# The straight turn of the inverse inside SBUF, and a last stage of 64-row, 32-column tiles, in a gated mix of an S4 convolution and a dense block

## The chip, the cores and the metric

One core of a Trainium2 chip runs the whole kernel. The metric is the device time of one execution in microseconds. Five engines work side by side, each through its own list of instructions in order: PE (products; PEld is its weight loads), DVE, ACT, POOL, and SP, which here only issues transfers. POOL issues transfers too. A transfer is asynchronous: what needs its data waits for a semaphore.

## The reference, cut to what matters

L = 2048 rows, D = 512 channels, N = 128 states, F = 1792 hidden units.

```python
g = sigmoid((u * gate_w).sum(-1, keepdims=True))
# A: S4 convolution
dt = exp(log_dt)[:, None]
K  = einsum("dn,dnl,dn->dl", Cc, exp((dt * A)[:, :, None] * arange(L)), dt * Bc).real
Yf = rfft(pad(u.T, 2 * L)) * rfft(pad(K, 2 * L))
a  = irfft(Yf, 2 * L)[:, :L].T + u * Dskip
# B: dense block
b  = gelu(u @ w1 + b1) @ w2 + b2
return g * a + (1 - g) * b
```

## The kernel before, in words

The transforms are done as products with small matrices, in three factors. The kernel has two functions with pools of their own. `front` computes the taps K, the first factors of both transforms and nearly all of the dense block; a planner orders it by due times. It leaves in DRAM `t2_d` (32 frequencies n, each a tile of 128 x 2 x 512: signal and taps after the first factors), in the output array the gated dense part of the 16 row tiles, and a list `late` of 14 entries of dense products (three PE products each) for the last two row tiles.

`conv` is written out by hand. It takes 16 steps s, two frequencies n = 2s and 2s+1 each. On PE a step issues `signal(s + 1)` (p2u), `taps(s + 2)` (p2k) and `inverse(s)` (pa); each is four products whose two tiles are halves of the array (64 columns for p2u and p2k, 64 rows for pa). ACT copies the taps out of PSUM (`k`), DVE multiplies both spectra in six operations of `product(s)` (`z`, `v`), PE's `inverse(s)` leaves one PSUM tile `pa` for each n, and `turn(s)` moves it on: ACT copies it to an SBUF tile `sa` (four of them in turn), and `settle` sends it towards `t3`, a tile of 128 partitions x 32 x 512. In `pa` the partition is the 32 places q for each of four parts j (which of two output halves, real or imaginary); in `t3` the partition is the frequency and part, with q along the free axis: 32 partitions' rows of `sa` become one row of `t3`.

Before, n = 0 to 27 go by DRAM: SP stores each `sa` to `t4_d[n]` (L1102), and after every eighth n (and after n = 27) POOL issues one gather from `t4_d` into rows of `t3` (L1105: three of 2 MB and one of 1 MB, the `GROUPS` table). The last four n go straight from `sa` to `t3`, one POOL transfer each, into four partitions 32 apart (L1107: rows 7, 39, 71 and 103 for the first).

SP's list holds, in the order of the program: the fetches of `t2` and of a matrix tile `cc` for each four n (12 tiles deep, `N_T2`), the 28 stores to `t4_d`, and from slot 32 on the loads of the dense part back into eight tiles `mo` (`dense`, in the same ring of 12).

In the last two steps there are no taps left, and `rest(4)` puts four `late` entries on PE ahead of each inverse; `rest(14)` takes what is left after the loop. Then comes the last stage: 16 row tiles t, each of two products with K = 128 rows and 64 columns (pb, L1164), one DVE operation that multiplies by the gate and adds the dense part in `mo` (L1166), and the store of two tiles at a time, of the last four singly.

Memory of the pools is handed on from `front` to `conv`: a tile that is laid over a tile of `front` waits for its last user. In PSUM, `pk` and `pa` have two buffers each, `pu` four; `pb` uses those of `pu`, `acc` of `rest` those of `pk`.

Of the kernel before, what the change touches and what calls it, by code (L numbers as in the profile page):

```python
# [9 lines left out]
F32 = mybir.dt.float32  # L10
# [3 lines left out]
ALU = mybir.AluOpType  # L14
# [3 lines left out]
P = 128  # L18
L = 2048
D = 512  # L20
# [44 lines left out]
D_COE = 0.99  # L65
D_OUT = -13.28
N_LATE = 2
N_REST = 4
N_T2 = 12
W_DVE = ((1, 0), (3, 0), (5, 0))  # L70

GROUPS = ((0, 8, 0, 4), (8, 8, 1, 4), (16, 8, 2, 4), (24, 4, 3, 8), (28, 1, 7, 32), (29, 1, 15, 32), (30, 1, 23, 32), (31, 1, 31, 32))
PI = float(np.pi)
TWO_PI = 2.0 * PI
TURN = 2.0**32
# [8 lines left out]
def slot_q():  # L84
    return [32 + m if m < 32 else 63 - m for m in range(64)]


def k0_order():
    return [8 * (n % 4) + n // 4 for n in range(32)]


def split12(v):
# [11 lines left out]
def constants():  # L104


    def om(e4):
        a = 2.0 * np.pi * (np.asarray(e4) % (4 * L)) / (4 * L)
        return np.cos(a), -np.sin(a)

    k0 = np.arange(32)
    p = np.arange(32)
    q = np.asarray(slot_q())
    k1 = np.arange(64)
    qn = np.arange(64)

    er, ei = om(4 * (64 * np.outer(p, k0) + 16 * p[:, None]))

    f1 = np.zeros((2, 32, 32, 2, 2))
    for i in range(2):  # L120
        f1[i, :, :, 0, i] = er
        f1[i, :, :, 1, i] = ei
    f1h, f1l = split12(np.concatenate([f1.reshape(64, P)] * 2, 0))


    g1 = np.zeros((2, 2, 32, 2, 32))
    for i in range(2):
        g1[i, 0, :, i] = er.T / L
        g1[i, 1, :, i] = ei.T / L
    g1 = g1.reshape(4, 32, 64)  # L130
    rows = np.zeros((P, 64))
    for first, count, at, step in GROUPS:
        for i in range(count):
            for j in range(4):
                rows[at + step * (4 * i + j)] = g1[j, k0_order()[first + i]]
    g1 = rows


    f2 = np.zeros((32, 2, 64, 2, 64))
    g2 = np.zeros((32, 2, 64, 64, 2))  # L140
    for k in range(32):
        er, ei = om(4 * (q[:, None] * k + 32 * np.outer(q, k1)) + q[:, None])
        f2[k, 0, :, 0], f2[k, 1, :, 0], f2[k, 0, :, 1], f2[k, 1, :, 1] = er, -ei, ei, er
        er, ei = om(4 * (qn[None] * k + 32 * np.outer(k1, qn)) + qn[None])
        g2[k, 0, :, :, 0], g2[k, 1, :, :, 0] = er, ei
        g2[k, 0, :, :, 1], g2[k, 1, :, :, 1] = -ei, er
    g2 = g2.reshape(32, P, 32, 2, 2).transpose(0, 1, 3, 4, 2)

    ko = k0_order()
    f2 = f2.reshape(32, P, P)[ko]  # L150
    g2 = g2[ko].reshape(16, 2, 2, 64, P).transpose(0, 2, 1, 3, 4).reshape(32, P, P)
    c2 = np.stack([f2, g2], 1).reshape(8, 4, 2, P, P).transpose(0, 3, 1, 2, 4)
    c1 = np.concatenate([f1h, f1l], 1)
    return (
        np.ascontiguousarray(c1, dtype=np.float32),
        np.ascontiguousarray(g1, dtype=np.float32),
        np.ascontiguousarray(c2, dtype=np.float32),
    )
# [105 lines left out]
def gated_mix(  # L264
# [18 lines left out]
    nc = tc.nc  # L283

    cp = ctx.enter_context(tc.tile_pool(name="cp", bufs=1))
    dr = ctx.enter_context(tc.tile_pool(name="dr", bufs=1, space=DRAM))

    dt_d = dr.tile([1, D], F32, name="dt_d")
    t2_d = dr.tile([32, P, 2, D], F32, name="t2_d")
    t4_d = dr.tile([32, P, D], F32, name="t4_d")  # L290

    half_pi = cp.tile([P, 1], F32, name="half_pi")
    nc.vector.memset(half_pi, PI / 2)
# [3 lines left out]
    gate = cp.tile([P, 2, 16], F32, name="gate")  # L297
# [731 lines left out]

    def conv(pool, ps, late):  # L1030

        t3 = pool.tile([P, 32, D], F32, name="t3", bufs=1)
        g1t = pool.tile([P, 64], F32, name="g1t", bufs=1)
        ko = k0_order()
        c4s, t2s = {}, {}

        def fetch(n):
            if n % 4 == 0:
                c4s[n // 4] = pool.tile([P, 4, 2, P], F32, tag="cc", name=f"cc{n}", bufs=3)
                nc.sync.dma_start(c4s[n // 4], c2[n // 4])  # L1040
            t2s[n] = pool.tile([P, 2, D], F32, tag="t2", name=f"t2{n}", bufs=N_T2)
            nc.sync.dma_start(t2s[n], t2_d[ko[n]])
            if n == 7:
                nc.sync.dma_start(g1t, g1)


# [19 lines left out]
        def signal(s):  # L1066
            pus[s] = []
            for c in range(2):
                pu = ps.tile([P, D], F32, tag="pu", name=f"p2u{s}{c}", bufs=4)
                pair(s, 0, c, pu)  # L1070
                pus[s].append(pu)

        def product(s):

            (ur, ui), (kr, ki) = pus.pop(s), fac.pop(s)
            z = [pool.tile([P, D], F32, tag=f"z{i}", name=f"z{s}{i}", bufs=1) for i in range(4)]
            v = [pool.tile([P, D], F32, tag=f"v{i}", name=f"v{s}{i}", bufs=2) for i in range(2)]
            nc.vector.tensor_mul(z[0], ur, kr)
            nc.vector.tensor_mul(z[1], ur, ki)
            nc.vector.tensor_mul(z[2], ui, ki)  # L1080
            nc.vector.tensor_mul(z[3], ui, kr)
            nc.vector.tensor_sub(v[0], z[0], z[2])
            nc.vector.tensor_add(v[1], z[1], z[3])
            prod[s] = v
# [10 lines left out]
                    r = slice(64 * i, 64 * i + 64)  # L1095
                    nc.tensor.matmul(pas[2 * s + i], w[r], v[c][r], start=(c == 0), stop=(c == 1))  # L1096

        def settle(n, sa):

            for first, count, at, step in GROUPS:  # L1100
                if count > 1 and first <= n < first + count:
                    nc.sync.dma_start(t4_d[n], sa)  # L1102
                    if n == first + count - 1:
                        rows = t4_d[first : n + 1].rearrange("n (j q) d -> (n j) q d", j=4)
                        nc.gpsimd.dma_start(t3[at:P:step], rows)  # L1105
                elif n == first:
                    nc.gpsimd.dma_start(t3[at:P:step], sa)  # L1107

        def turn(s):
            for n in (2 * s, 2 * s + 1):  # L1110
                sa = pool.tile([P, D], F32, tag="sa", name=f"sa{n}", bufs=4)
                nc.scalar.copy(sa, pas.pop(n))  # L1112
                settle(n, sa)

        accs, mos = {}, {}

# [18 lines left out]

        for n in range(N_T2):
            fetch(n)
        nxt = N_T2
        taps(0)
        signal(0)  # L1140
        taps(1)
        for s in range(16):

            for n in range(nxt, min(2 * s + N_T2, 40)):
                (fetch if n < 32 else dense)(n if n < 32 else n - 32)
                nxt = n + 1
            product(s)
            if s + 1 < 16:
                signal(s + 1)
            if s + 2 < 16:  # L1150
                taps(s + 2)
            else:
                rest(N_REST)
            inverse(s)
            turn(s)
        rest(14)
        for s in range(N_LATE):
            z = mos[7][:, s]
            nc.vector.scalar_tensor_tensor(z, accs[s], gate[:, 1, 14 + s : 15 + s], z, ALU.mult, ALU.add)

        for t in range(16):
            pb = ps.tile([P, D], F32, tag="pu", name=f"pb{t}", bufs=4)
            for b in range(2):
                nc.tensor.matmul(pb[64 * b : 64 * b + 64], g1t, t3[:, 2 * t + b], start=True, stop=True)  # L1164
            z, g = mos[t // 2][:, t % 2], gate[:, 0, t : t + 1]
            nc.vector.scalar_tensor_tensor(z, pb, g, z, ALU.mult, ALU.add)  # L1166
            if t >= 12:
                nc.sync.dma_start(out[t], z)
            elif t % 2 == 1:
                nc.sync.dma_start(out[t - 1 : t + 1].rearrange("s p d -> p s d"), mos[t // 2])  # L1170

    ctx.enter_context(tc.manual_schedule())
    keep = ctx.enter_context(tc.tile_pool(name="keep", bufs=1))
# [17 lines left out]
def layout(inputs):  # L1191

    x = np.asarray(inputs["A_u"]).reshape(L, D)
    xpq = x.reshape(32, 64, D)
    qs = np.asarray(slot_q())

    xl = xpq[:, qs].reshape(32, 2, 16, 2, D).transpose(2, 3, 1, 0, 4).reshape(16, P, D)

    xs = xpq.reshape(32, 16, 4, D).transpose(1, 2, 0, 3).reshape(16, P, D)
    xt = xs.reshape(NSB, SB, 4, P).transpose(0, 3, 2, 1)  # L1200

    order = np.arange(D).reshape(4, 2, NCH, 2, 8).transpose(0, 2, 3, 1, 4).reshape(D)
    names = ["A_A_re", "A_A_im", "A_B_re", "A_B_im", "A_C_re", "A_C_im"]
    prm = np.stack([np.asarray(inputs[n])[order].T for n in names], 1)
    w1 = np.asarray(inputs["B_w1"]).reshape(4, P, NF, P).transpose(2, 1, 0, 3).reshape(NF, P, D)
    c1, g1, c2 = constants()
    return {
        "xl": xl,
        "xs": xs,
        "xt": xt,  # L1210
        "prm": prm,
        "logdt": np.asarray(inputs["A_log_dt"])[order].reshape(1, D),
        "dskip": np.asarray(inputs["A_Dskip"])[order].reshape(16, 4, 8).transpose(1, 0, 2).reshape(4, P),
        "w1": w1,
        "b1": np.asarray(inputs["B_b1"]).reshape(NF, P).T,
        "w2": np.asarray(inputs["B_w2"]),
        "b2": np.asarray(inputs["B_b2"]).reshape(1, D),
        "gw": np.asarray(inputs["gate_w"]).reshape(1, D),
        "c1": c1,
        "g1": g1,  # L1220
        "c2": c2,
    }
# [24 lines left out]
```

## Time and profile before

| | us |
|---|---|
| runs | 575.47, 573.12, 574.60 (median 574.6) |
| profiled execution | 573.21 |
| its span | 571.4 |
| end of `front` on PE | 433.7 |
| last inverse (pa) | 532.24 to 534.16 |
| pb, last stage | 550.16 to 567.09 |

Share of the span: PE 95% busy, DVE 79%, ACT 63%, POOL 6%; the mean granted clock of PE is 0.975. The costliest groups of the page belong to `front`. Those of `conv`, as groups by line (line, engine, operation, out<-in, count, then busy us, mean ns of one, idle time before and its releaser):

```profile
L1112 ACT COPY sa<-pa 128x512 f32<-128x512 f32 x32 | 17.7, 588 | 36.8 <-PE pa L1096 21.1
L1055 PE MATMUL p2k<-t,cc 128*64 128x512 f32 x128 | 35.4, 613 | 3.0 <-DMA t<-t_d 1.7
```

The issues of transfers by kind on the page (line, engine, operation, count, KB each, median us from issue to landing); in such rows `t` stands for `t2` tiles and for `t3`, `t_d` for `t2_d` and `t4_d`, since the digits are left out:

```profile
t<-t_d SPq DMA_DIRECT2D x32, 512.0 KB, 7.9
t_d<-sa SPq DMA_DIRECT2D x28, 256.0 KB, 6.9
mo<-out_dram SPq DMA_DIRECT2D x8, 512.0 KB, 9.6
```

Each fp32 product appears as two PE records. Two records of two halves of the array overlap, so a row's count times its mean is more than its busy time. The time that an engine stood idle is put down to what ended last; whether it cost anything depends on whether the engine bounds that stage.

### The profile page before, as it was taken

What the parts mean: (1) busy time and instruction counts of PE and PEld (TensorE: products, weight loads), DVE (VectorE), ACT (ScalarE), POOL (GpSimd) and SP (SyncE); (2) the same over time, 40 slices, a digit from 0 to 9 for tenths busy, and PEclk for the clock granted to TensorE, in tenths of its full rate; (3) what the DMA queues carried; (4) which work ended last, traced back from release to release, by engine and by line L of the source; (5) the groups of instructions that cost most, each with busy time, mean ns of one, the idle gap of its engine ahead of it and who ended that gap; (6) DMA issues with size and microseconds to landing.
All of it is one profiled execution on the core that took longest, in us unless ns stands there. A gap on an engine that the chain in (4) does not pass through costs nothing.

```text
span 571.4 us, 11957 instructions
## 1 busy us (share of the span) xinstructions
PE 541.3 (95%) x4746; PEld 403.8 (71%) x4746; DVE 449.4 (79%) x844; ACT 361.8 (63%) x606; POOL 32.2 (6%) x69
## 2 busy tenths in 40 slices
PE   7859999999999999999999999999998999999646
PEld 7738878888887888888888889898884333324412
DVE  5899998998989989998998898988512766675116
ACT  4998656899676799987669857477443334333100
POOL 2000000000000000000120201101010000000200
PEclk9969999999999999999999999999998999999959
DMA  8868735232864232649531358223269899999846
GB/s 267 306 216 304 240 111 186 75 130 86 255 209 167 95 130 93 201 141 252 137 82 33 95 122 156 75 38 80 35 143 334 320 322 396 380 420 452 230 97 258
DMA packets 77396, 109.50 MB, mean 192 GB/s; under 512 B 39014, under 2 KB 42218, under 8 KB 77228
## 3 DMA queue, kind: packets, MB, share of 16 engines
q1 hardware_dynamic: 71484, 87.89, 45.2%
q0 software_dynamic: 5856, 20.85, 14.6%
q8 instruction: 37, 0.61, 0.4%
q14 instruction: 19, 0.16, 0.1%
HBM read 63.09 MB, written 44.57 MB: 188 GB/s over the span
## 4 chain that ended last, share of the span: by engine, by line
PE 77%; DMA 14%; DVE 2%; ACT 2%; SPq 1%; issue 1%; POOL 0%; POOLq 0%; ACTq 0%
PE pk L647 11%; PE acc L905 9%; PE ph L857 9%; PE ph L859 8%; PE ph L858 8%; PE acc L907 8%; PE acc L906 8%; DMA t_d<-sa 5%; PE pu L388 4%; PE p2k L1055 3%; PE pb L1164 3%; DMA t<-t_d 3%; PE pa L1096 3%; PE p2u L1055 3%; DMA t<-sa 2%; DMA ld<-in_xt_dram 2%
## 5 line engine op out<-in xcount | busy, mean ns | idle before, releaser
L857 PE MATMUL ph<-xh,wh 128*128 128x256 f32 x448 | 128.0, 286 | 1.5 <-DVE wh L736 1.5
L859 PE MATMUL ph<-xh,wl 128*128 128x256 f32 x448 | 127.0, 283 | 0.6 <-DVE wl L740 0.5
L858 PE MATMUL ph<-xlo,wh 128*128 128x256 f32 x448 | 126.5, 282 | 0.0
L857 PEld LDWEIGHTS ph<-xh,wh 128*128 128x128 f32 x448 | 85.1, 190 | 7.5 <-issue 4.0
L905 PE MATMUL acc<-wh,hh 128*128 128x512 f32 x210 | 87.8, 418 | 0.4 <-ACT hh L877 0.4
L858 PEld LDWEIGHTS ph<-xlo,wh 128*128 128x128 f32 x448 | 85.1, 190 | 1.7
L859 PEld LDWEIGHTS ph<-xh,wl 128*128 128x128 f32 x448 | 85.1, 190 | 1.2 <-DVE wl L740 1.2
L906 PE MATMUL acc<-wl,hh 128*128 128x512 f32 x210 | 83.2, 396 | 0.0
L907 PE MATMUL acc<-wh,hl 128*128 128x512 f32 x210 | 82.9, 395 | 0.0
L874 ACT ACTIVATE ph<-ph,b1t 128x256 f32<-128x256 f32 x112 | 50.6, 452 | 28.7 <-PE ph L859 26.9
L647 PE MATMUL pk<-y,xc 128*32 128x64 f32 x2048 | 61.5, 290 | 0.0
L647 PEld LDWEIGHTS pk<-y,xc 128*32 128x32 f32 x2048 | 57.2, 136 | 4.0 <-issue 2.5
L905 PEld LDWEIGHTS acc<-wh,hh 128*128 128x128 f32 x210 | 39.8, 190 | 19.8 <-issue 11.9
L887 DVE TENSOR_TENSOR hl<-ph,hh 128x512 fp32r<-128x512 f32 (+1 forms) x62 | 38.2, 618 | 13.1 <-ACT hh L877 12.5
L907 PEld LDWEIGHTS acc<-wh,hl 128*128 128x128 f32 x210 | 39.8, 190 | 9.7 <-DVE hl L887 0.8
L611 DVE TENSOR_TENSOR y<-y,ea 128x64 f32<-128x64 f32 (+4 forms) x80 | 45.3, 566 | 0.4
L906 PEld LDWEIGHTS acc<-wl,hh 128*128 128x128 f32 x210 | 39.9, 190 | 5.8
L666 ACT COPY sk<-pu 128x512 f32<-128x512 f32 x32 | 33.9, 1129 | 15.5 <-PE pu L388 15.3
L1112 ACT COPY sa<-pa 128x512 f32<-128x512 f32 x32 | 17.7, 588 | 36.8 <-PE pa L1096 21.1
L877 ACT CAST hh<-ph 128x512 fp32r<-128x512 f32 (+1 forms) x62 | 33.0, 532 | 10.9 <-PE acc L906 9.1
L456 DVE TENSOR_TENSOR xt<-xc,zz 128x256 f32<-128x256 f32 (+2 forms) x48 | 37.2, 775 | 1.9 <-ACT xc L582 1.6
L1055 PE MATMUL p2k<-t,cc 128*64 128x512 f32 x128 | 35.4, 613 | 3.0 <-DMA t<-t_d 1.7
(138 smaller groups left out, 891.5 us busy)
## 6 DMA issues: line engine op xcount, KB each, us to landing
t<-t_d SPq DMA_DIRECT2D x32, 512.0 KB, 7.9
t_d<-st SPq DMA_DIRECT2D x32, 256.0 KB, 3.3
t_d<-sk SPq DMA_DIRECT2D x32, 256.0 KB, 4.2
t_d<-sa SPq DMA_DIRECT2D x28, 256.0 KB, 6.9
ld<-in_xt_dram SPq DMA_DIRECT2D x16, 256.0 KB, 3.9
xh_d<-xh SPq DMA_DIRECT2D x8, 512.0 KB, 3.8
xl_d<-xlo SPq DMA_DIRECT2D x8, 512.0 KB, 5.5
ux<-in_xl_dram SPq DMA_DIRECT2D x16, 256.0 KB, 3.4
```

The lines of the kernel that those rows point to most:

```text
L456: vec(2 * m, lambda: vv.tensor_mul(t, a, br), due, [ka, *kb], [kt])
L611: nc.vector.tensor_mul(both(n, 64 - 3 * n, n), both(0, 64 - n, n), an)
L647: nc.tensor.matmul(pks[q][32 * j : 32 * j + 32, gg], x[:, r, :, ch], y[:, r, :, ch], start=(r == 0), stop=(r == 1), skip_group_check=True,)
L857: nc.tensor.matmul(p, h, xh[xk][:, d], start=(d == 0), stop=False)
L858: nc.tensor.matmul(p, h, xlo[xk][:, d], start=False, stop=False)
L859: nc.tensor.matmul(p, lo, xh[xk][:, d], start=False, stop=(d == 3))
L874: nc.scalar.activation(phs[q][:, n], phs[q][:, n], AF.Gelu_apprx_tanh, bias=b1t[:, f : f + 1])
L887: nc.vector.tensor_sub(lo, phs[q][:, 0:nf], hi.bitcast(F32))
L905: nc.tensor.matmul(a, h, wh[1][w], start=start, stop=False)
L906: nc.tensor.matmul(a, h, wl[1][w], start=False, stop=False)
L907: nc.tensor.matmul(a, l, wh[1][w], start=False, stop=(j == 3))
L1055: nc.tensor.matmul(out[64 * i : 64 * i + 64], w, t2s[n][:, r], start=True, stop=True)
```

## The change

- **The turn.** `t4_d`, the `GROUPS` table and `settle` are gone, and with them 28 stores on SP and four gathers on POOL. Each n goes straight from `sa` to `t3` by two POOL transfers of 128 KB, one for each half of `sa` (64 partitions), into two rows of `t3` that lie 4 apart: rows 64i + seat(n) and 64i + seat(n) + 4. There are 64 such transfers.
- **Buffers.** `sa` and `z` are four fixed tiles each (`sas`, `zs`). `t3` and `g1t` are allocated after the fourth fetch, not first. `g1t` is 32 columns wide and loaded at n = 11.
- **The rest.** `rest` takes 3 entries, and only in step 15; 11 are left for after the loop.
- **The last stage.** Eight pairs m of row tiles. For each, eight products: 64 rows (half i of `t3` goes to tile i of the pair) by 32 columns (place b). Five of the 16 tiles (`ASIDE`) are not evacuated by DVE: ACT multiplies by the gate into a `z` tile and POOL adds it to `mo`.
- **Layouts.** The host's order of `xs`, of the rows of g1 and of the output follow the new tiles.

```diff
-N_REST = 4
+N_REST = 3
-GROUPS = ((0, 8, 0, 4), (8, 8, 1, 4), (16, 8, 2, 4), (24, 4, 3, 8), (28, 1, 7, 32), (29, 1, 15, 32), (30, 1, 23, 32), (31, 1, 31, 32))
+ASIDE = (2, 5, 8, 11, 14)
+def seat(n):
+    return 8 * (n % 4) + n // 4 % 4 + 32 * (n // 16)
...
+    rows = np.zeros((2, 64, 32))
+    for n, k in enumerate(k0_order()):
+        rows[:, seat(n)] = er.T[k] / L
+        rows[:, seat(n) + 4] = ei.T[k] / L
+    g1 = rows.reshape(P, 32)
...
-    t4_d = dr.tile([32, P, D], F32, name="t4_d")
...
     def conv(pool, ps, late):
-        t3 = pool.tile([P, 32, D], F32, name="t3", bufs=1)
-        g1t = pool.tile([P, 64], F32, name="g1t", bufs=1)
+        sas = [pool.tile([P, D], F32, name=f"sa{k}", bufs=1) for k in range(4)]
+        zs = [pool.tile([P, D], F32, name=f"z{k}", bufs=1) for k in range(4)]
...
-            if n == 7:
+            if n == 11:
                 nc.sync.dma_start(g1t, g1)
...
-            z = [pool.tile([P, D], F32, tag=f"z{i}", name=f"z{s}{i}", bufs=1) for i in range(4)]
+            z = zs
...
         def turn(s):
             for n in (2 * s, 2 * s + 1):
-                sa = pool.tile([P, D], F32, tag="sa", name=f"sa{n}", bufs=4)
+                sa = sas[n % 4]
                 nc.scalar.copy(sa, pas.pop(n))
-                settle(n, sa)
+                for i in range(2):
+                    at = 64 * i + seat(n)
+                    nc.gpsimd.dma_start(t3[at : at + 5 : 4], sa[64 * i : 64 * i + 64])
...
         for n in range(N_T2):
             fetch(n)
+            if n == 3:
+                t3 = pool.tile([P, 32, D], F32, name="t3", bufs=1)
+                g1t = pool.tile([P, 32], F32, name="g1t", bufs=1)
...
-            else:
+            if s == 15:
                 rest(N_REST)
...
-        for t in range(16):
-            pb = ps.tile([P, D], F32, tag="pu", name=f"pb{t}", bufs=4)
-            for b in range(2):
-                nc.tensor.matmul(pb[64 * b : 64 * b + 64], g1t, t3[:, 2 * t + b], start=True, stop=True)
-            z, g = mos[t // 2][:, t % 2], gate[:, 0, t : t + 1]
-            nc.vector.scalar_tensor_tensor(z, pb, g, z, ALU.mult, ALU.add)
-            if t >= 12:
-                nc.sync.dma_start(out[t], z)
-            elif t % 2 == 1:
-                nc.sync.dma_start(out[t - 1 : t + 1].rearrange("s p d -> p s d"), mos[t // 2])
+        for m in range(8):
+            pbs = [ps.tile([P, D], F32, tag="pu", name=f"pb{m}{i}", bufs=4) for i in range(2)]
+            for b in range(4):
+                for i in range(2):
+                    r = slice(64 * i, 64 * i + 64)
+                    nc.tensor.matmul(
+                        pbs[i][32 * b : 32 * b + 32], g1t[r], t3[r, 4 * m + b], start=True, stop=True
+                    )
+            for i in range(2):
+                t = 2 * m + i
+                z, g = mos[m][:, i], gate[:, 0, t : t + 1]
+                if t in ASIDE:
+                    a = zs[ASIDE.index(t) % 4]
+                    nc.scalar.mul(a, pbs[i], g)
+                    nc.gpsimd.tensor_add(z, z, a)
+                else:
+                    nc.vector.scalar_tensor_tensor(z, pbs[i], g, z, ALU.mult, ALU.add)
+                if m >= 6:
+                    nc.sync.dma_start(out[t], z)
+            if m < 6:
+                nc.sync.dma_start(out[2 * m : 2 * m + 2].rearrange("s p d -> p s d"), mos[m])
```

The order of `front` is the same on every engine. Two places of `conv` follow as the built programs have them; "waits" names the semaphores of an instruction: PE_49, DVE_49 and Pool_49 are those of engines, DMAHW and DMASW those of transfers of SP and POOL. SP's list where `conv` begins, before (t20, t21... are the `t2` tiles):

```order
L1040 DMA cc0_4844<-in_c2_dram 128x1024 [waits DMAHW7_49,DVE_49,Pool_49]
L1042 DMA t20_4846<-t2_d_61 128x1024 [waits DMAHW4_49,DMAHW3_49,DMAHW5_49,DMAHW2_49,DMAHW6_49,DMAHW1_49,DMAHW0_49]
L1042 DMA t21_4848<-t2_d_61 128x1024 [waits DMASW6_49,DMASW5_49,PE_49]
L1042 DMA t22_4850<-t2_d_61 128x1024
L1042 DMA t23_4852<-t2_d_61 128x1024
```

And the same place after the change:

```order
L1039 DMA cc0_4849<-in_c2_dram 128x1024 [waits DVE_49,DMAHW7_49,PE_49,Pool_49]
L1041 DMA t20_4851<-t2_d_61 128x1024 [waits DMAHW4_49,DMAHW3_49,DMAHW5_49,DMAHW2_49,DMAHW6_49,DMAHW1_49,DMAHW0_49]
L1041 DMA t21_4853<-t2_d_61 128x1024
L1041 DMA t22_4855<-t2_d_61 128x1024
L1041 DMA t23_4857<-t2_d_61 128x1024
```

The fetch of t21 no longer waits for PE; the matrix tile cc0 does. The PE instruction that t21 waited for is the last hidden product of `front` (L859); the one that cc0 waits for is the last taps product (L645 after the change, L647 before), which the profile has at 411.

PE's list around the first inverse of step 14 (pa140, pa141), before; acc0 is a `late` row tile:

```order
L1133 MATMUL acc0_5549<-wh13_133,xlo00_121 128x512
L1096 MATMUL pa140_5562<-v140_5535,cc28_5303 128x512
L1096 MATMUL pa141_5563<-v140_5535,cc28_5303 128x512
L1096 MATMUL pa140_5562<-v141_5536,cc28_5303 128x512
L1096 MATMUL pa141_5563<-v141_5536,cc28_5303 128x512
L1131 MATMUL acc0_5549<-wh14_134,hh0_151 128x512
```

After the change:

```order
L1054 MATMUL p2u151_5489<-t230_5314,cc28_5272 64x512
L1054 MATMUL p2u151_5489<-t231_5316,cc28_5272 64x512
L1095 MATMUL pa140_5492<-v140_5478,cc28_5272 128x512
L1095 MATMUL pa141_5493<-v140_5478,cc28_5272 128x512
L1095 MATMUL pa140_5492<-v141_5479,cc28_5272 128x512
L1095 MATMUL pa141_5493<-v141_5479,cc28_5272 128x512
L1122 MATMUL acc0_5512<-wh10_129,xh00_118 128x512
```

The inverse of step 14 now stands right behind p2u of step 15, and the first `late` entry behind it.

More of the change, by code (lines that the diff above doesn't have):

```diff
@@ L123, in constants @@
     f1h, f1l = split12(np.concatenate([f1.reshape(64, P)] * 2, 0))
[L126 to L136, printed above, removed]
+    rows = np.zeros((2, 64, 32))
[3 more added lines that the diff above has]
+    g1 = rows.reshape(P, 32)
     f2 = np.zeros((32, 2, 64, 2, 64))
@@ L1096, in inverse @@
                     nc.tensor.matmul(pas[2 * s + i], w[r], v[c][r], start=(c == 0), stop=(c == 1))
[L1098 to L1107, printed above, removed]
         def turn(s):
             for n in (2 * s, 2 * s + 1):
-                sa = pool.tile([P, D], F32, tag="sa", name=f"sa{n}", bufs=4)
+                sa = sas[n % 4]
                 nc.scalar.copy(sa, pas.pop(n))
-                settle(n, sa)
+                for i in range(2):
+                    at = 64 * i + seat(n)
+                    nc.gpsimd.dma_start(t3[at : at + 5 : 4], sa[64 * i : 64 * i + 64])
         accs, mos = {}, {}
@@ L1197, in layout @@
     xl = xpq[:, qs].reshape(32, 2, 16, 2, D).transpose(2, 3, 1, 0, 4).reshape(16, P, D)
-    xs = xpq.reshape(32, 16, 4, D).transpose(1, 2, 0, 3).reshape(16, P, D)
+    xs = xpq.reshape(32, 8, 4, 2, D).transpose(1, 3, 2, 0, 4).reshape(16, P, D)
     xt = xs.reshape(NSB, SB, 4, P).transpose(0, 3, 2, 1)
@@ L1244 @@
     o = np.asarray(r.results[0]["out_0_dram"])
-    o = o.reshape(16, 4, 32, D).transpose(2, 0, 1, 3).reshape(1, L, D)
+    o = o.reshape(8, 2, 4, 32, D).transpose(3, 0, 2, 1, 4).reshape(1, L, D)
     return np.ascontiguousarray(o)
```

## The prediction

> **What bounds the kernel now.** I read the page's 40 slices first (here PE's, busy share in tenths), then the chain of waits, then single stretches. All times are of the profiled execution: 573.21 us, span 571.4, so 1.8 us lie around the span; it is 1.4 under the median of 574.6.
>
> ```profile
> PE   7859999999999999999999999999998999999646
> ```
>
> PE is at 9 nearly everywhere but in three of the last four slices. The change touches the last 138 us, so I followed the chain there.
>
> ```profile
> 433.74 3.61 DMA t<-t_d
> 437.39 2.82 PE p2k L1055 x5
> ...
> 447.51 1.92 PE pa L1096 x8
> 449.43 1.87 PE p2u L1055 x8
> 451.30 1.72 PE p2k L1055 x8
> ...
> 537.84 12.13 DMA t<-sa
> 549.96 0.20 issue
> 550.16 16.93 PE pb L1164 x64
> 567.11 0.75 DVE mo L1166
> ```
>
> PE ends the front at 433.7, waits, but for one product at 434.84, for the taps tiles to 437.39, and then repeats pa, p2u, p2k: 1.92 + 1.87 + 1.72 = 5.51 us a step, bound by PE. Before the last stage stands a wait of 12 us for the turned inverses; then 17 us of products (pb), one evacuation and 3.5 us of stores end the span. The clock and the transfers by stretch (columns after the stretch: its length; busy time of PE, PEld, DVE, ACT, POOL with counts; granted clock; DMA share; GB/s):
>
> ```profile
> 437.40:447.40 10.00, 10.00 (x38) 3.05 (x38) 5.79 (x10) 2.93 (x5) 0.00 (x0) 0.86 1.02 408
> 447.40:502.50 55.10, 55.10 (x243) 17.65 (x242) 37.10 (x62) 22.48 (x40) 1.08 (x2) 1.00 0.95 352
> 541.00:549.00 8.00, 0.00 (x0) 0.00 (x0) 0.00 (x0) 0.00 (x0) 0.00 (x0) 0.59 0.86 131
> 550.20:556.20 6.00, 6.00 (x16) 1.89 (x18) 2.11 (x3) 0.00 (x0) 0.00 (x0) 0.50 0.11 43
> 556.20:567.10 10.90, 10.87 (x52) 3.71 (x48) 9.15 (x13) 0.00 (x0) 0.00 (x0) 1.00 0.74 279
> 565.30:567.90 2.60, 1.77 (x10) 0.34 (x6) 2.25 (x3) 0.00 (x0) 0.00 (x0) 1.00 0.98 373
> ```
>
> After both waits PE runs at a lower clock: 0.86 in the first ten us, 0.50 in the first six of the last stage. In 541 to 549 nothing computes.
>
> **Start of the stage (-3.0).** The second tile's fetch stands behind PE's last front product; the queue's waits and PE's rows:
>
> ```profile
> SPq L1042 <- PE ph L859: 3.5, 1, 3.5
> 434.84 1.04 PE L1055 MATMUL p2k<-t,cc 128*64 128x512 f32 x2 [1.13 <-ACT hh L877]
> 437.39 1.12 PE L1055 MATMUL p2k<-t,cc 128*64 128x512 f32 x2 [1.51 <-DMA t<-t_d]
> ```
>
> In the order after, that fetch has no PE wait (t3, allocated first before, now comes after four fetches; its place is no longer asked for early). The tile can be there when PE frees; PE's first product still waits for ACT, to 434.84. So PE runs on there instead of pausing to 437.39: 2.55. The ten us at 0.86 may then run at 1.00: up to 1.4 more. Bounds: -1.3 (the tile still lands late, clock unchanged) to -4.0. I take -3.0, near the wait itself, with a third of the clock.
>
> **Fewer transfers inside the loop (-1.4).** One step has a stall:
>
> ```profile
> 511.99 3.11 PE L1055 MATMUL p2k<-t,cc 128*64 128x512 f32 x8 [0.18 <-DMA t<-t_d]
> 518.83 1.89 PE L1055 MATMUL p2k<-t,cc 128*64 128x512 f32 x8
> ```
>
> 3.11 - 1.89 + 0.18 = 1.4. Each step before moves two 512 KB fetches, 512 KB out to t4_d and as much back; after, the fetches and 512 KB straight. At 352 GB/s and 0.95 share (447.4 to 502.5) the transfers were nearly full, and a quarter of the bytes goes. I take the whole stall; bounds 0 and -1.4.
>
> **Remainder of the dense part (-3.6).** Before, rest(4) stands ahead of inverse(14) and of inverse(15):
>
> ```profile
> 524.44 0.50 PE L1131 MATMUL acc<-wh,xh 128*128 128x512 f32 x1
> 527.38 1.99 PE L1096 MATMUL pa<-v,cc 64*128 64x512 f32 x8
> 529.30 0.50 PE L1131 MATMUL acc<-wh,hh 128*128 128x512 f32 x1
> 532.24 1.99 PE L1096 MATMUL pa<-v,cc 64*128 64x512 f32 x8
> 534.16 0.50 PE L1131 MATMUL acc<-wh,xh 128*128 128x512 f32 x1
> ```
>
> Each costs 527.38 - 524.44 = 2.94, 0.69 for each entry between its first and last. After, one rest(3) is left, 2.3, ahead of inverse(15) alone. What the two covered is DVE's product, six operations of 0.69 = 4.1:
>
> ```profile
> 522.57 1.94 PE L1055 MATMUL p2u<-t,cc 128*64 128x512 f32 x8
> L1083 DVE TENSOR_TENSOR v<-z,z 128x512 f32<-128x512 f32 x16 | 11.0, 685 | 0.0
> ```
>
> In the times of before, product(14) may run from 518.9, where p2u(14) ended, to 523.0: inverse(14) starts bare at 524.44. Product(15) runs from 524.44 to 528.6, while PE does inverse(14) (1.92) and rest(3) (2.3) to 528.7: just covered; without rest(3) PE would stand 2.2 there. So the last inverse ends 5.9 - 2.3 = **3.6 earlier**, with the terms above at 534.16 - 8.0 = 526.2. The other 11 entries follow it, 11 x 0.69 + 0.3 = 7.9: PE is busy to 534.1, over most of the landing below.
>
> **Turn (the 12 us gap).** Before, the last four n and the last gather:
>
> ```profile
> 535.22 0.49 POOL L1105 DMA_DIRECT2D t<-t_d  x1 [12.09 <-DMA t_d<-sa]
> 535.75 2.75 POOL L1107 DMA_DIRECT2D t<-sa  x4
> DMA to landing us min/median/max: 12.1/12.8/13.6
> xh<-xh_d POOLq DMA_DIRECT2D x8, 512.0 KB, 4.0
> L1112 ACT COPY sa<-pa 128x512 f32<-128x512 f32 x32 | 17.7, 588 | 36.8 <-PE pa L1096 21.1 <-DMA t_d<-sa 15.5
> ```
>
> After the last inverse at 526.2: two copies of 0.59 on ACT to 527.5; POOL issues two transfers per n at 2.75 / 4 = 0.69, the last at 528.8. No gather stands ahead of them. The landing of 128 KB into two partitions is in no row. Lower bound 4.0 (a 512 KB POOL transfer into 128 partitions); upper 13.6 (straight from sa, behind the 1 MB gather: in 541 to 549 alone 1 MB at 131 GB/s). I take 6: the load ahead of it is gone, but two partitions are far narrower than 128. So products may start at 534.8, with PE done at 534: start S = 535, against 550.16, **15.2 earlier**. With 4.0 PE's 534.1 decides, with 13.6 S is 542.4. Of the 15.2, 8.0 are the three terms above and 7.2 the gap itself.
>
> [...]
>
> In the loop each sa tile is written again two steps (11.0 us) later; the issue time is 4 x 0.69 = 2.75 of 5.5 us. Neither delays PE as long as a landing stays under about 11.0 - 0.59 - 0.69 = 9.7. Waiting on ACT, k copies would queue behind, then DVE's product, then PE.
>
> **Last stage.** Before from 550.16 to 571.4: 21.2. The rows, products before and the nearest narrow ones:
>
> ```profile
> L1164 PE MATMUL pb<-t,g1t x64: 592/592/1116, 550.2 to 566.5; 128*64 128x512 f32 x64
> L647 PE MATMUL pk<-y,xc 128*32 128x64 f32 x2048 | 61.5, 290 | 0.0
> 556.81 11.05 DVE L1166 SCALAR_TENSOR_TENSOR mo<-pb,gate,mo 128x512 f32<-128x512 f32 x13 [0.47 <-PE pb L1164]
> L812 POOL MEMSET ld<- 33x512 f32 x1 | 0.6, 552 | 0.0
> out_dram<-mo SPq DMA_DIRECT2D x4, 256.0 KB, 2.5
> ```
>
> Before, every product is two records, and two 64-column tiles run side by side: p2k's 8 records take 1.72, so a pair takes 0.43, at clock 1.00. After, 64 products are 128 records. If all eight 64 x 32 tiles run side by side: 16 rounds x 0.43 = 6.9 us; if four do, 13.8; only two, 27.5. I take eight: pa's row halves take 1.92 for 8 records, so they pair too, and the 32-column products of L647 sum to 2048 x 0.290 = 594 in 61.5 busy, so many stand side by side; nothing shows both kinds at once. S follows a busy PE without a pause over 1 us, so I take clock 1.00; with the six us at 0.50 of before, 3.0 at most come back.
>
> Then evacuation: a bare 0.75 each on DVE before (13 in 11.05, some behind PE). Eleven remain, 8.3, while ACT and POOL take five. ACT's copy is 0.59. A POOL add over 128x512 is in no row: lower bound 0.55 (a POOL fill of 33x512), upper 1.7 (five of them then last as long as DVE's eleven, so beyond it they would decide). I take 1.2, hidden beside DVE. POOL's order has one library reload ahead of its first addition, with no row for its cost; POOL has nothing to do from 528.8 to S + 3, and these 9 us hide it up to that length.
>
> The stores, 16 tiles of 256 KB = 4.2 MB, decide: the first pair is ready at S + 0.9 (two rounds) + 2 x 0.75 = S + 2.4; at the 373 GB/s of 565.3 to 567.9 they take 11.2; the last one lands 2.5 after its issue: S + 16.1, **5.1 less than 21.2**. If evacuation decided instead, S + 0.9 + 8.3 + 3.5 = 12.7 is the lower bound. The span ends at 535 + 16.1 = 551.1. Sum: 15.2 + 5.1 = 20.3; 573.21 - 20.3 = 552.9. Against runs whose median lies 1.4 higher I write 553.5.
>
> **The rivals.** **Products only in pairs (0.08).** If row tiles and column tiles do not combine, the products last 27.5: 535 + 27.5 + 0.75 + 3.5 = 566.8, time 568.5. For it: no row has both kinds of tile at once. Against: each kind alone runs side by side.
>
> **Narrow transfers hold the sa tiles, mildly (0.15).** A landing of x us in the loop costs (1.28 + x - 11.0) / 2 a step over 14 steps, and at the end x - 6. At 10 that is 2 + 4, at 11.4 it is 11.8 + 5.4: 559 to 571. For it: 12.1 to 13.6 in the only row of this kind. Against: that row stood behind 1 MB of gather, with all four sent at once.
>
> **The same, strongly: slower (0.08).** The same sum eats all 20.3 at **x = 11.8**: 7 x (11.8 - 9.7) + 5.8 = 20.5. The loop of copy, issue and landing is then 13.1 for two steps, so 6.5 a step instead of 5.5, and PE waits for pa's release by ACT. Beyond it the kernel is slower than before: at the row's 12.8, 21.7 + 6.8 = 28.5 on 552.9, 581. The row as it stands lies past the point; what speaks against is as above, and that a quarter fewer bytes move beside it.
>
> **It moves nothing (0.05).** The gap stays as another wait (late landings alone, or stores that begin no sooner): within 0.5% of 574.6. The order shows each n issued in its own step, so only a landing near 11.7 could do it.
>
> **How the numbers follow.** Forecast 548 to 559: 0.62; better than 548: 0.02. The range reaches over the mild rival nearly whole and the pairs: 548 to 569 leaves out 0.02 + 0.08 + 0.05 and a quarter of the mild one, 0.19. Over 0.5% (about what a measurement of this kernel can tell from no change): faster 0.87, within 0.05, slower 0.08.
>
> **What would show it.** In the profile after: PE's first conv product near 434.8 and no wait for t to 437; no stall of 3 us in the loop; the last pa end near 526; transfers of t<-sa landing in about 6 us; pb starting near 535 with clock 1.00 and lasting about 9; the stores at 370 GB/s or more to the end. What would make it wrong: ACT's sa copies waiting on t<-sa in the loop, a pb stage of over 15 us, POOL's additions ending after DVE's, or PE waiting after 534 for a landing.

## The result, and the profile after

The changed kernel takes 602.92 us in the median (597.46 to 610.11, four runs) against 574.41 before (573.12 to 575.47). Two of its four runs (606.93 and 610.11) are in a slower state, as is one execution each of four_4_spread (1705.81) and four_4_rot (1705.88) below, so every ratio leaves such runs out: here 597.46 and 598.91 make 1.0415 times the time before, 95% interval 1.0372 to 1.0458, or 23.8 us more. The profiled execution took 598.91 us with a span of 597.1.

The page after, PE's busy tenths and its granted clock in 40 slices:

```profile
PE   7959999999999999999999999999999788986874
PEclk9869999999999999999999999999999769996888
```

Before, PE stood still in two places of `conv`, ahead of and behind the loop. Now the loop itself has holes, from slice 32 on, and the clock falls with them (digits 7 and 6 in slices 32 and 33). The chain of waits shows what fills them:

```profile
446.34 1.92 PE pa L1095 x8
...
456.63 22.53 DMA t<-sa
...
492.82 14.25 DMA t<-sa
...
521.14 14.60 DMA t<-sa
...
537.57 20.56 DMA t<-sa
...
561.13 8.64 DMA t<-sa
...
570.75 6.54 DMA t<-sa
...
577.34 1.04 PE pb L1160 x2
```

Before, this chain was PE for step after step, 5.51 us each, up to 477, and then the fetches and stores. After, it goes from a straight transfer to ACT's copy, a few PE products, and to the next transfer; `t<-sa` is in it with 49.8% of the time from 425 to 600. Next the groups by line, the landings of the straight transfers (issued in line 1104), and the page's issues:

```profile
L1101 ACT COPY sa<-pa 128x512 f32<-128x512 f32 x32 | 18.2, 587 | 79.7 <-DMA t<-sa 61.6
L1095 PE MATMUL pa<-v,cc 64*128 64x512 f32 x128 | 43.8, 693 | 16.0 <-ACT sa L1101 16.0
```

```profile
DMA to landing us min/median/max: 6.4/11.2/25.1
```

```profile
t<-t_d SPq DMA_DIRECT2D x32, 512.0 KB, 10.2
t<-sa POOLq DMA_DIRECT2D x64, 128.0 KB, 11.2
```

ACT's copy into an `sa` tile waits for that tile's two transfers of two steps ago, 61.6 us in all; PE then waits for the `pa` tile that ACT hasn't emptied. The transfers land after 11.2 us in the median and after 25.1 at worst. The fetches take longer too: 10.2, and 7.9 before. Two stretches say how the transfer engines do beside this (columns as in the prediction):

```profile
456.60:479.20 22.60, 16.87 (x54) 4.72 (x50) 9.33 (x16) 3.92 (x7) 4.64 (x8) 0.79 0.99 261
536.00:558.00 22.00, 13.90 (x32) 4.23 (x32) 3.75 (x6) 4.20 (x8) 5.28 (x8) 0.70 1.02 206
```

Their share is 0.99 and 1.02, at 261 and 206 GB/s; before, the loop had 352 GB/s at 0.95. In these stretches they are always busy and move less, so each byte takes longer: SP's queue needed 85.0% of their time for 17.27 MB in 447.4 to 502.5 before, and 71.4% for 4.75 MB in the first stretch here, about a quarter more for a byte. POOL's narrow transfers took 27.6% for 1.14 MB. That, not the number of bytes, is what had to be explained.

### The profile page after: what moved, and what is told of

Same layout as the page of the kernel before. It is cut to its first block, busy times and chain, and to the rows that moved or that the text cites. A ratio compares the mean times of both kernels' runs of the same rounds, so it can differ in the third digit from the quotient of the medians.

```text
span 597.1 us, 12150 instructions
## 1 busy us (share of the span) xinstructions
PE 553.7 (93%) x4810; PEld 406.8 (68%) x4810; DVE 445.9 (75%) x839; ACT 364.7 (61%) x611; POOL 76.0 (13%) x130
## 4 chain that ended last, share of the span: by engine, by line
PE 72%; DMA 20%; ACT 2%; SPq 2%; issue 1%; POOL 1%; DVE 1%; POOLq 0%; ACTq 0%
DMA t<-sa 15%; PE pk L645 10%; PE acc L903 9%; PE ph L855 8%; PE ph L857 8%; PE ph L856 8%; PE acc L905 8%; PE acc L904 7%; PE pu L386 5%; PE pa L1095 2%; PE p2u L1054 2%; PE p2k L1054 2%; PE pb L1160 2%; DMA ld<-in_xs_dram 1%; DMA y<-in_w_dram 1%; SPq L679 1%
## 5 line engine op out<-in xcount | busy, mean ns | idle before, releaser
L1101 ACT COPY sa<-pa 128x512 f32<-128x512 f32 x32 | 18.2, 587 | 79.7 <-DMA t<-sa 61.6
L1077 DVE TENSOR_TENSOR z<-p2u,k 128x512 f32<-128x512 f32 x16 | 11.1, 691 | 67.7 <-PE p2u L1054 64.2
L645 PE MATMUL pk<-y,xc 128*32 128x64 f32 x2048 | 61.5, 290 | 0.0
L645 PEld LDWEIGHTS pk<-y,xc 128*32 128x32 f32 x2048 | 57.2, 136 | 4.0 <-issue 2.5
L1095 PE MATMUL pa<-v,cc 64*128 64x512 f32 x128 | 43.8, 693 | 16.0 <-ACT sa L1101 16.0
L1104 POOL DMA_DIRECT2D t<-sa x64 | 42.2, 665 | 100.1 <-ACT sa L1101 75.2
L1095 PEld LDWEIGHTS pa<-v,cc 64*128 64x128 f32 x128 | 15.3, 203 | 42.5 <-ACT sa L1101 25.6
## 6 DMA issues: line engine op xcount, KB each, us to landing
t<-t_d SPq DMA_DIRECT2D x32, 512.0 KB, 10.2
t<-sa POOLq DMA_DIRECT2D x64, 128.0 KB, 11.2
```

Source lines behind the costliest of these rows:

```text
L645: nc.tensor.matmul(pks[q][32 * j : 32 * j + 32, gg], x[:, r, :, ch], y[:, r, :, ch], start=(r == 0), stop=(r == 1), skip_group_check=True,)
L1104: nc.gpsimd.dma_start(t3[at : at + 5 : 4], sa[64 * i : 64 * i + 64])
```

## The experiments

Theory A said that the turn costs all of it, B that other parts do. Within A: the transfers are narrow (N), they meet the fetches (C), there are too many (T), they are only late and four `sa` tiles are too few (Q), or the place of their rows counts (P; later E: which transfer writes which row). "Landing" is the median from issue to landing of the straight transfers, in us; times are medians, ratios with their intervals where a run was timed in rounds.

| run | what differs | us | ratio to before | landing |
|---|---|---|---|---|
| turn_only | before, with the new turn | 613.8 | 1.0672 (1.0608 to 1.0735) | 12.9 |
| four_4 | before, one transfer for each n, 4 rows 4 apart, side by side | 602.4 | 1.0505 (1.0469 to 1.0541) | 14.2 |
| four_4_sa7 | the same, seven sa tiles | 604.4 | 1.0523 (1.0449 to 1.0598) | 25.8 |
| four_32 | the same as four_4, rows 32 apart | 675.2 | 1.1707 (1.1604 to 1.1811) | 24.8 |
| four_4_spread | the same as four_4, four n in different quarters | 569.8 | 0.9915 (0.9885 to 0.9945) | 9.4 |
| four_4_rot | the same, quarters shifted by one n | 595.5 | 1.0359 (1.0325 to 1.0392) | 13.0 |
| two_aligned | turn_only, pairs of rows in another order | 587.4 | 1.0215 (1.0162 to 1.0267) | 10.1 |
| start_rest | before, with buffers and rest of the change | 569.9 | 0.9942 (0.9921 to 0.9964) | 12.4, last four |
| old_turn3 | after, with the turn of before | 569.1 | 0.9926 (0.9893 to 0.9960) | 12.6, last four |
| spread_start_rest | four_4_spread and start_rest together | 564.0 | 0.9820 (0.9788 to 0.9851) | 9.3 |

**The turn alone, and all but the turn.** The kernel before, with

```diff
-                settle(n, sa)
+                for i in range(2):
+                    at = 64 * i + seat(n)
+                    nc.gpsimd.dma_start(t3[at : at + 5 : 4], sa[64 * i : 64 * i + 64])
```

and the 128 x 64 matrix `g1` with its rows in the order of `seat`.

> The kernel before with the new turn alone (two transfers of 128 KB for each n, rows 4 apart); last stage, rest and allocation as before. Theory A, the turn costs all that was lost: the other parts of the change gained about 2.6 (start) + 3.6 (rest) + 1.4 (last stage, 19.8 against 21.2), so this should be slower still than the changed kernel: about 610 us, ACT's sa copies waiting 60 us or more on t<-sa. Rival B, the loss comes from the new last stage, the rest or the buffers: then this is at or under 575 us and ACT does not wait on t<-sa.

613.8 us: the turn alone costs 40 us, and ACT waits 69.9 on t<-sa:

```profile
L1105 ACT COPY sa<-pa 128x512 f32<-128x512 f32 x32 | 18.2, 586 | 88.8 <-DMA t<-sa 69.9 <-PE pa L1100 18.9
```

A holds. (The parts don't add up: the turn's 40 and the gain of 3 to 4 found below would make 36 or 37, and the change lost 23.8. What the other parts save behind the slow turn wasn't taken apart.) The reverse took three runs. The first gave each group of n two gathers, one for each half of the rows:

> The changed kernel with the turn of before (stores to DRAM, gathers; two gathers a group, one for each half of rows). Theory A: start 2.6, rest 3.6 and last stage 1.4 to 5 are kept, and the wait ahead of the last stage is again some 12 us: 563 to 567 us. Rival B (the loss is in the other parts): 590 us or more.

It took 590.5 us (1.0313, 1.0277 to 1.0348), and seemed to speak for B. Its chain says otherwise:

```profile
474.22 15.41 DMA t<-t_d
...
501.50 18.51 DMA t<-t_d
```

Two fetches of 512 KB, issued at 474.22 and 501.50, stood 15 and 18 us behind gathers that write only one half of the partitions, issued at 472.65 and 501.18. The second had one gather again, but two stores for each n:

> The changed kernel with the turn of before, and one gather for a group again (DRAM holds a group's 32 rows in the order of t3: two stores of 128 KB for each n, one gather over all 128 partitions, rows 4 apart), since the two gathers in one half of the rows held the fetches up for 15 and 18 us. Theory A (the turn costs all that was lost, the other parts gain 8 to 11): 563 to 567 us, no wait for t<-t_d over 3 us in the loop. Rival B (the other parts cost time, as the 590 us of the last run could say): 585 us or more.

It took 579.2 us (1.0078, 1.0046 to 1.0109): its chain goes through stores `t_d<-sa` (there are 56) of 10.0 and 8.7 us, and its last inverse begins at 537.44, against 527.09 in the third run below. Both had put a cost of their own in. The third took the turn of before word for word and let the output be another (t3's rows belong elsewhere); beside it ran the buffers and the rest alone:

> The changed kernel with the turn of before word for word (28 stores, four gathers of whole groups); the last stage then reads rows that belong elsewhere, so the output differs. The two runs with two gathers or two stores for each group added transfers and SP slots of their own; here nothing is added. Theory A: start and rest as in the run with these alone, and the last stage 3 us shorter (18.1 in the last run against 21.2): 563 to 566 us. Rival B (the fixed tiles or the last stage cost time in the loop): 574 us or more.

> The kernel before with the buffers and the rest of the change alone: t3 allocated after the fourth fetch, fixed sa and z tiles, rest(3) in the last step only. By the prediction's terms the start gives 3.0 and the last inverse comes 3.6 earlier; both are kept if the wait ahead of the last stage still begins at the last inverse: 574.2 - 6.6 = 567 to 569 us. Rival: SP's queue and the gathers (fetches, stores and loads in one order) decide when the last rows are there, not PE, so the earlier inverse is lost in a longer wait: 571 to 574 us.

569.1 and 569.9 us. By the ratios, all but the turn gains 4.2 and 3.3 us, half or less of what was expected; in neither run does one of the two forecasts hold. Why the rest gave less, start_rest shows, in PE's timeline and the chain:

```profile
527.06 1.99 PE L1096 MATMUL pa<-v,cc 64*128 64x512 f32 x8
```

```profile
522.23 10.78 DMA t_d<-sa
...
536.14 11.88 DMA t<-sa
548.02 0.20 issue
548.22 15.62 PE pb L1167 x64
```

The last inverse ends at 529.1, 5.1 earlier than before; the last stage starts 1.9 earlier. The chain runs from step 13's copies through the store of n = 27 and the gather behind it to the last landing: the last inverse isn't on it, as the rival said.

**Fetches left out.** The changed kernel with

```diff
-            t2s[n] = pool.tile([P, 2, D], F32, tag="t2", name=f"t2{n}", bufs=N_T2)
-            nc.sync.dma_start(t2s[n], t2_d[ko[n]])
+            if n < N_T2:
+                ...
+            else:
+                t2s[n] = t2s[n % N_T2]
```

> The changed kernel without the 20 fetches of t2 after the twelfth; steps past the sixth use the tiles that lie there, so the output differs. Theory N, a transfer into two partitions is slow by itself: landings stay at 11 us in the median, ACT's copies wait on t<-sa as before, 590 us or more. Theory C, what slows it is the fetches beside it: landings fall to 5 to 7 us (the last transfers of the changed kernel, with nothing beside them, landed in 6.4), steps take 5.5 us, about 553 us.

576.1 us in a single execution, landing 9.8, ACT's wait 41.5: between the two. Where the wait lies, three stretches show:

```profile
447.00:480.00 33.00, 33.00 (x142) 10.50 (x142) 21.46 (x36) 13.45 (x24) 15.89 (x24) 1.00 0.73 174
480.00:505.00 25.00, 24.02 (x104) 7.56 (x100) 15.38 (x26) 9.30 (x17) 10.52 (x16) 1.00 0.61 140
505.00:535.00 30.00, 25.40 (x87) 7.71 (x85) 13.31 (x22) 7.71 (x14) 8.59 (x14) 0.89 0.99 205
```

Without the fetches the straight transfers hardly hold the loop up before 505. They do behind it, where the eight loads of the dense part run (512 KB each, issued from 500.8 on) and the transfer engines are full.

**Number, distance, depth.** On the kernel before, `settle` was replaced by one transfer for each n:

```diff
+                nc.gpsimd.dma_start(t3[16 * (n // 4) + n % 4 : 16 * (n // 4) + n % 4 + 13 : 4], sa)   # four_4
+                nc.gpsimd.dma_start(t3[n:P:32], sa)                                                   # four_32
-                sa = pool.tile([P, D], F32, tag="sa", name=f"sa{n}", bufs=4)
+                sa = pool.tile([P, D], F32, tag="sa", name=f"sa{n}", bufs=7)                          # four_4_sa7
```

> As turn_only, but one transfer of 256 KB for each n into four partitions 4 apart. Each partition still gets 64 KB. Theory N (64 KB into each partition is the limit): landing and time as in turn_only within 1%. Rival T (the number of transfers, 64, and what each costs all engines, is the limit): half as many, so the wait on t<-sa falls by half or more and the time by 10 us or more.

> One transfer of 256 KB for each n into four partitions 32 apart instead of 4 apart, all else as in the run with four partitions 4 apart (602.4 us, landing 14.2). [...] Rival N (what counts is 64 KB into each of few partitions, wherever they lie): within 1% of 602.

> One transfer for each n into four partitions 4 apart, with seven sa tiles instead of four, so that up to seven transfers are on the way. Theory Q (the transfers are only late, and four tiles are too few to cover it): 7 x 256 KB in 14.2 us is 129 GB/s where 5.5 us a step ask for 95, so ACT's wait on t<-sa goes and the time falls to 575 to 580 us. Rival S (they go no faster than about 74 GB/s in all, 4 x 256 KB in 14.2 us): the landing grows to 20 us or more and the time stays at 595 us or more.

four_4 took 602.4: half the transfers give 11 us of 40, and ACT's wait falls from 69.9 to 60.4, not by half: neither N nor T. four_4_sa7 stands on the side of its rival S: with 7 instead of 4 on the way the landing grows from 14.2 to 25.8 and the time stays, so more tiles only lengthen the line. four_32 is the surprise: the same bytes, transfers and tiles take 73 us more, landing 24.8. In 455 to 500, four_4 and then four_32:

```profile
455.00:500.00 45.00, 39.69 (x134) 11.69 (x132) 21.07 (x35) 11.72 (x21) 7.80 (x12) 0.85 1.00 221
```

```profile
455.00:500.00 45.00, 30.01 (x94) 8.29 (x90) 14.84 (x24) 7.13 (x13) 4.66 (x7) 0.86 1.04 150
```

The transfer engines are full in both (1.00, 1.04) and move 221 and 150 GB/s. A packet takes longer in the second: in 455 to 505 those of POOL's queue took 34.1% of the 16 engines' time for 2957 packets in four_4 and 36.6% for 1803 in four_32, so 0.09 and 0.16 us for one, and those of SP's queue 65.8% for 2145 and 67.7% for 1431, 0.25 and 0.38 us for one. The landings are 14.2 and 24.8 us. In both kernels the rows of four n that follow each other are neighbours.

**Rows of neighbours apart.** Then the rows of four n went to different quarters, 0, 16, 64, 80:

```diff
+def base(n):
+    return 16 * (n % 2) + 64 * (n // 2 % 2) + n // 4 % 4 + 32 * (n // 16)
...
+                nc.gpsimd.dma_start(t3[base(n) : base(n) + 13 : 4], sa)
```

> One transfer for each n into four partitions 4 apart, all else as before, but the rows of four n that follow each other lie in different quarters (0, 16, 64, 80 and so on) instead of side by side. [...] Rival S (a straight transfer is limited elsewhere, in its reads or its start, about 74 GB/s in all): within 2% of 602.

569.8 us, landing 9.4: the straight turn is as good as the old one, a little better. But P alone can't be all: the change, too, has 16 rows on the way 4 or more apart (0, 4, 64, 68, 8, 12 and so on), and loses. What differs is which transfer writes where. So the quarters were shifted by one n (16, 64, 80, 0), and, on turn_only, the 64 transfers took their pairs of rows in the order 0, 8, 16, 24, 64, 72, 80, 88 and again instead of 0, 64, 8, 72 and so on. By P neither should matter, since the rows on the way lie as far apart as before; by E both should:

```diff
+    m = (n + 1) % 4
+    return 16 * (m % 2) + 64 * (m // 2) + n // 4 % 4 + 32 * (n // 16)          # four_4_rot
+def place(t):
+    return 8 * (t % 4) + 64 * (t // 4 % 2) + t // 8 % 4 + 32 * (t // 32)       # two_aligned, t = 2n + i
```

> As the run with one transfer for each n and the rows of four n in different quarters (569.8 us), but each n goes to the quarter of the next one (16, 64, 80, 0): the rows written at the same time lie exactly as far apart. [...]

> [...] Rival T (64 transfers cost too much whatever rows they have): 600 us or more.

The shift alone costs 26 us: 595.5. The order alone gives 26 back: 587.4 against 613.8. E has the direction here and not the size: the author's estimate for the new order was a landing under 9 us and 570 to 580 us, and the landing is 10.1. The landings of the shifted kernel are from a second execution:

> The same kernel as four_4_rot (595.5 us), whose profiled execution had a PE that took three times as long in every product; this one is for the landings. Theory E: a median of 12 us or more, against 9.4 with the quarters not shifted. If it is 9.4 too, the 25 us of the shift come from somewhere else than the landings.

Its time was 594.8, its landing 13.0, as E expected. In 455 to 500 stands, for four_4_spread, then for the shifted kernel:

```profile
455.00:500.00 45.00, 41.86 (x174) 13.08 (x172) 26.09 (x43) 16.42 (x29) 9.84 (x15) 0.96 0.89 288
```

```profile
455.00:500.00 45.00, 42.31 (x157) 12.89 (x157) 23.60 (x39) 13.47 (x24) 8.03 (x12) 0.92 1.00 237
```

288 GB/s at a share of 0.89, and 237 at 1.00: the same transfers, and each byte takes about 1.4 times as much of the engines' time (1.00/237 against 0.89/288). Last, both without the fetches:

> One transfer for each n, rows in different quarters, without the 20 fetches of t2 after the twelfth (later steps use the tiles that lie there, so the output differs). All theories: landing 6 to 8 us, ACT's wait on t<-sa under 10 us, about 565 us.

> The same with the quarters shifted by one, also without these fetches. [...] Theory E2 (the shift hurts by itself, fetches or not): landing 10 us or more, 10 us more than spread_no_fetch.

571.3 and 574.4 us, landings 8.8 and 9.7. Three stretches of each, spread first:

```profile
447.00:480.00 33.00, 33.00 (x146) 10.41 (x140) 23.36 (x39) 13.19 (x24) 6.76 (x10) 1.00 0.64 185
480.00:505.00 25.00, 25.00 (x112) 8.04 (x112) 16.32 (x27) 10.15 (x18) 6.48 (x10) 1.00 0.58 148
505.00:535.00 30.00, 30.00 (x124) 11.99 (x121) 16.85 (x28) 10.06 (x18) 6.88 (x11) 1.00 0.79 242
```

```profile
447.00:480.00 33.00, 33.00 (x142) 10.41 (x140) 21.36 (x36) 13.55 (x24) 7.16 (x11) 1.00 0.65 182
480.00:505.00 25.00, 25.00 (x112) 8.02 (x110) 17.74 (x30) 10.27 (x18) 6.33 (x10) 1.00 0.68 158
505.00:535.00 30.00, 27.31 (x100) 9.44 (x98) 15.33 (x25) 8.01 (x14) 5.40 (x8) 0.89 0.98 212
```

Up to 501 the only wide transfers issued beside it are the matrix tiles, and the shifted kernel's PE is as busy as the other's. Then the eight loads of the dense part are issued, 512 KB each over 128 partitions (from 503.1 and 501.5 on), and the shift costs again: share 0.98 instead of 0.79, PE busy for 27.31 instead of 30.00 us. From the first inverse to the last, the shift costs 21.4 us with the fetches (111.9 against 90.5) and 6.5 without (91.3 against 84.8). So the shift costs less by itself than the 10 us that E2 took, and most where wide transfers run beside it. What makes one order slower than the other there, no run shows. These two are single executions, and that their times come within 1% of each other is partly luck: spread_no_fetch started late, with the clock at 8 tenths in slices 31 and 32 of its page where four_4_spread has 9, and its first inverse at 450.81 instead of 446.81.

**The version that beats both.** The spread turn with start_rest:

> One transfer for each n with the rows in different quarters, together with the buffers and the rest of the change (each alone: 569.8 and 569.9). If both gains add, 573.1 - 3.3 - 3.3 = 566.5 us; if the straight turn has taken the gathers out of the way of the earlier inverse, more: 562 us. Rival: the last landing (9.4 us in the median) sets the end of both, 569 to 570 us.

564.0 us, 0.982 of before (0.9788 to 0.9851): the gains add, and a little over. Its PE timeline at the end is:

```profile
528.35 1.99 PE L1100 MATMUL pa<-v,cc 64*128 64x512 f32 x8
541.74 15.65 PE L1160 MATMUL pb<-t,g1t 128*64 128x512 f32 x64 [3.69 <-issue]
```

The `late` products fill the time from 530.3 to 538.0, and the last stage starts 8.4 us earlier than before, after a wait of 3.7 instead of 12. This is the forecast's picture with wider transfers, in an order that fits.

## Why the prediction was wrong

The forecast, 553.5 us with a range of 548 to 569 and a chance of 0.87 for faster, failed at one step: the landing. "I take 6", with 4.0 and 13.6 as bounds, "Neither delays PE as long as a landing stays under about 9.7". Measured: 6.4 at best, 11.2 in the median, 25.1 at worst. 6 us is near what a transfer takes with little beside it, as the last two do (6.54 and 7.54). The bound was a little wide too: in the step with its copies at 562.51 to 563.58 and its four issues at 563.39 to 566.01, the last issue starts 1.8 us behind its own copy, so 11.0 - 0.59 - 1.8 = 8.6 is nearer; two_aligned's 10.1 lies over it.

The row that spoke for the slow rival, 12.1 to 13.6 for straight transfers, was explained away by the 1 MB gather ahead of it. The reason for slowness that the prediction named, destinations far narrower than 128, wasn't the main one: four_4_spread writes only four rows at a time and lands in 9.4, and with two rows the order alone gives back 26 of the 40 us. What else runs during a landing stood there only as an argument ("a quarter fewer bytes move beside it") and had no term in the sum; which transfer writes which row had none either.

- **Start, -3.0:** right. From the end of the front's products (433.71 before, 435.13 after) to the first inverse (447.51, 446.34) PE takes 13.8 and 11.2 us: 2.6 less, at clock 1.00 in 437.5 to 447.5, where before had 0.86 in its first ten us.
- **Stall, -1.4, by fewer bytes:** wrong. Fewer bytes left the transfer engines full where PE waits (0.99 and 1.02), and from the first inverse to the last the loop took 118.4 us instead of 84.8.
- **Rest, -3.6:** nearly right for the inverse (5.1 earlier in start_rest, of which 1.9 stand at its first inverse, 445.50 instead of 447.44, and 3.2 are left for the rest), and worth it only where the turn is straight: with gathers 1.9 of it arrived at the last stage. Behind the straight turn that fits, start and rest together bring about 1% (0.9915 to 0.9820).
- **Last stage, -5.1:** 1.4 of it came. PE doesn't fall to pairs:

```profile
577.34 1.04 PE L1160 MATMUL pb<-t,g1t 64*32 64x512 f32 x2 [3.01 <-DMA t<-sa]
579.04 10.22 PE L1160 MATMUL pb<-t,g1t 64*32 64x512 f32 x126 [0.66 <-issue]
581.06 1.41 DVE L1171 SCALAR_TENSOR_TENSOR mo<-pb,gate,mo 128x512 f32<-128x512 f32 x2 [5.95 <-PE pb L1160]
588.17 1.28 POOL L1169 TENSOR_TENSOR mo<-mo,z 128x512 f32<-128x512 f32 x1 [0.42 <-DVE mo L1171]
590.16 1.26 POOL L1169 TENSOR_TENSOR mo<-mo,z 128x512 f32<-128x512 f32 x1 [0.71 <-ACT z L1168]
```

  126 of 128 records in 10.22 us rule the rival of pairs out (27.5), and the POOL addition takes 1.26 to 1.28 where 1.2 was taken. But the stage starts after a wait, the clock is at 0.83 in 577.3 to 587.4, and the first evacuation comes 3.7 us after the first product and not 0.9. POOL's last addition ends at 591.4, later than DVE's at 590.3, which the prediction had named as a sign of being wrong, and the stores stand behind it: 597.1 - 577.3 = 19.8 instead of 16.1, where before took 21.2. With the turn of before it is 566.4 - 548.5 = 17.9, against 567.9 - 548.2 = 19.7 in start_rest: a gain of 1.8.
- **The rival that came true,** "The same, strongly: slower" (0.08), had its point at a landing of 11.8 us. Its mechanism is the one seen, ACT's copies waiting on t<-sa. Its size fails: at the median of 11.2 its sum gives 552.9 + 7 x 1.5 + 5.2 = 569. A copy waits for the later of two transfers, and landings of 14 to 22 us in the chain weigh more than the median does.

Open is why 64 transfers of two rows in the fitting order take 587.4 and 32 of four rows 569.8, 14 of the 40 us; that a step's last issue comes late, as above, is argued and not tested. The traces add that in 430 to 600 POOL's queue took 25.1% of the engines' time for 9.02 MB in two_aligned and 20.2% for 8.79 MB in four_4_spread, with 16480 and 7760 packets under 512 B in all queues. The changed kernel itself was not run in another order. Nor is it tested how the new last stage would do behind a straight turn that fits: its halves of rows can't be had by one transfer of four rows 4 apart.

## What to carry to other kernels

Here the turn inside SBUF was priced by which transfer writes which rows (613.8 or 587.4 us, 569.8 or 595.5) and by what else runs then, more than by its bytes: full transfer engines at falling GB/s (221 in four_4 and 150 in four_32, at shares of 1.00 and 1.04) were the sign. Before giving up a way through DRAM, try the straight one with few, wider transfers, and with two orders of the destination rows; here one order gains 0.9% and another loses 3.6%. Take the slow row of a kind of transfer as it stands until a run shows what made it slow.

## What the runs showed of the hardware

- Four destination partitions 32 apart instead of 4 apart: 675.2 against 602.4 us, 150 against 221 GB/s in the same stretch with the engines full.
- The same rows, assigned to transfers one place further: 595.5 against 569.8, and the wide loads beside them land in 21.6 us instead of 13.1 (the shifted kernel, then four_4_spread):

```profile
mo<-out_dram SPq DMA_DIRECT2D x8, 512.0 KB, 21.6
mo<-out_dram SPq DMA_DIRECT2D x8, 512.0 KB, 13.1
```

- With gathers of 1 MB that each write one half of the partitions, 512 KB fetches landed after 15.4 and 18.5 us in the chain (old_turn); with gathers of the same bytes over all partitions, before, after 13.0 at worst.
- Row tiles and column tiles do combine: 126 records of 64 x 32 in 10.22 us are 0.081 each. If a record takes 0.43 us, as a pair of p2k's does, about five stood side by side, an estimate. Evacuation held them: PE's weight loads waited 3.1 us for DVE and 2.4 for ACT.
